# A top-32 mask made by a GpSimd compare in the first 48 slots instead of by ScalarE's bound and Relu

## The chip, the cores and the metric

The kernel runs on one core of a Trainium2 chip. Five engines work side by side: TensorE (PE in the profile; PEld is its weight load), VectorE (DVE), ScalarE (ACT), GpSimd (POOL) and SyncE (SP, which only issues transfers here). The metric is the device time of one execution in microseconds (us). The kernel before took 1338.02 us in the median of three runs (1337.96 to 1338.56).

## The reference

Two blocks follow each other. The first is attention over 8 batches, 8 heads, 576 positions and 64 columns per head, in which each row keeps only its 32 largest scores:

```
scores = scale * q @ k.T                        # 576 x 576 per head
kth    = the 32nd largest score of each row
scores = where(scores >= kth, scores, -1e9)
attn   = exp(scores - max(scores));  attn /= sum(attn) + 1e-9
out    = attn @ v
```

The outputs of all heads are laid side by side (4608 rows of 512). The second block is a mixture of 8 experts: each row goes to the one expert with the largest gate logit, `relu(x @ w1[e]) @ w2[e]`, and the result is multiplied by the gate's probability.

## The kernel before, in words

**Slots.** The attention is cut into 144 slots, 18 per batch. A slot holds two tiles (m = 0 and 1) of 128 query rows by 576 keys. The loop `loop()` goes through the slots; in each of them every engine gets its instructions in the order in which the loop writes them (TensorE, ScalarE and VectorE by a manual schedule, GpSimd by `in_turn`). Four units of two heads make a batch.

**The work of one slot**, with the lines of the kernel before:

- TensorE multiplies q and k (L292) and ScalarE copies the scores out into the tile `s`, 128x2x576 (L299). This is done three slots ahead (`AHEAD = 3`); `s` has four buffers.
- VectorE finds the 32 largest of each row. For the *next* slot it folds the 576 scores into halves by a pairwise maximum and minimum, `h` (L306) and `l` (L308), and later once more, `few` (L314) and `hl` (L316). These four are TENSOR_TENSOR operations with two inputs. `search()` then takes the eight largest of the set-aside parts (L345), and four rounds of MAX8 and MATCH_REPLACE8 (L354, L362) on the folded row give the 32 largest, `tops`. In the instruction order of VectorE, one slot goes: h, l, six MAX8 of L345, three rounds, few, hl, the last MAX8 of each of the two tiles, and then h of the next slot. The 32nd value, `thr = tops[:, :, 31]`, is the row's threshold.
- ScalarE turns the threshold into a bound, `low = thr * 2^120` (L371), and `depths()` makes `w = relu(low - s * 2^120)` for each of the two tiles (L387): 0 for a score that is kept, a huge number for one that isn't.
- GpSimd subtracts: `w = s - w` (`less()`, L396, two per slot). It also makes `nbias`, minus the row's maximum times the scale, behind the first round of MAX8 (L358), and `doubt` (L377), by which the fold is verified at the end.
- ScalarE takes the exponential of `w` with `nbias` as bias and adds up the row (L404). TensorE transposes it a slot later (L415), ScalarE copies that out (L422), and the product with v follows when a head pair is complete.
- When a unit is complete, GpSimd scales its rows and gate logits: xl (L487), lg (L489, L490 or L492) and x (L500). This falls into ten of the first 48 slots. At the end of a batch it scatters the rows to memory by expert (L567).

`w` has three buffers, `few` three.

**The experts.** The blocks of the second part (L893, L910) are strewn between the slots as rows arrive; the first can only start when two batches are through, after about slot 48. What is left of them runs on TensorE behind the last slot.

Of the kernel before, what the change touches and what calls it, by code (L numbers as in the profile page):

```python
# [9 lines left out]
F32 = mybir.dt.float32  # L10
I32 = mybir.dt.int32
AF = mybir.ActivationFunctionType
ALU = mybir.AluOpType
# [5 lines left out]
TOP_K = 32  # L19
NEG = -3.0e38  # L20
STEEP = 2.0 ** 120
EPS = 1e-9


# [18 lines left out]
def kernel(  # L43
# [47 lines left out]
    nc = tc.nc  # L91
    B, U, P, _ = qk.shape
# [23 lines left out]
    scale = float(D) ** -0.5  # L116
# [13 lines left out]
    k = SimpleNamespace()  # L130
# [116 lines left out]
    def in_turn(put):  # L247

        if not k.exact:
            tc.keep_in_program_order(put)  # L250
        return put
# [68 lines left out]
    def tick():  # L320

        while aside:
            if next(aside[0], "end") != "end":
                return
            aside.pop(0)
# [4 lines left out]
        if steps in aside:  # L330
            aside.remove(steps)

    def search(tiles, s, f, then=lambda: None):

        m_all = range(2)
        tops = k.small.tile([P, 2, TOP_K], F32, name="tops", bufs=4)
        if k.exact:
            src = [s[:, m, :, :].rearrange("p j k -> p (j k)") for m in m_all]
            width = S
        else:  # L340
            src = [f.few[:, m, 0:QF] for m in m_all]
            width = LW
            for m in m_all:
                for j, away in enumerate((f.l[:, m, :], f.hl[:, m, 0:QF // 2], f.hl[:, m, QF // 2:QF])):
                    nc.vector.max(out=f.few[:, m, QF + 8 * j:QF + 8 * j + 8], in_=away)  # L345
        scr = k.att.tile([P, 2, width], F32, name="scr", bufs=1)
        nbias = k.small.tile([P, 2], F32, name="nbias", bufs=3)
        R = TOP_K // 8

        for r in range(R):  # L350
            if r == R - 1:
                then()
            for m in m_all:
                nc.vector.max(out=tops[:, m, r * 8:(r + 1) * 8], in_=src[m])  # L354
                if r:
                    tick()
            if r == 0:
                in_turn(nc.gpsimd.tensor_scalar_mul(nbias, tops[:, :, 0], -scale))  # L358
            if r < R - 1:
                for m in m_all:  # L360
                    first = r == 0 and not k.exact
                    nc.vector.match_replace(  # L362
                        out=src[m] if first else scr[:, m, :], in_to_replace=tops[:, m, r * 8:(r + 1) * 8],
                        in_values=src[m], imm_value=NEG,
                    )
                    if r:
                        tick()
                    src[m] = f.few[:, m, :] if first else scr[:, m, :]
        thr = tops[:, :, TOP_K - 1]
        low = k.small.tile([P, 2], F32, name="low", bufs=3)  # L370
        nc.scalar.activation(low, thr, AF.Copy, scale=STEEP)  # L371

        def doubts():
            n, i = tiles[0]
            at = n.b * U + n.u
            over = doubt[:, at:at + 2, 2 * NC, :] if tails(tiles) else doubt[:, at, 2 * i:2 * i + 2, :]
            k.last_pool = in_turn(nc.gpsimd.tensor_tensor(  # L377
                over, f.few[:, :, QF + 7:LW:8], _inner(thr, NL), op=ALU.subtract
            )).ins

        return low, nbias, doubts

    def depths(s, low):

        w = k.att.tile([P, 2, S], F32, name="w", bufs=1 if k.exact else 3)
        for m in range(2):
            nc.scalar.activation(  # L387
                w[:, m, :], s[:, m, :, :].rearrange("p j k -> p (j k)"), AF.Relu,
                scale=-STEEP, bias=low[:, m:m + 1],
            )  # L390
        return w
# [78 lines left out]
    def divisors(n):  # L470
        rz = rz_of[n.u % 2]
        nc.scalar.activation(rz[:, 0:NT], n.z, AF.Copy, bias=EPS)
        if n.u % 2:
            nc.scalar.activation(rz[0:ST, NT:NT + 1], n.z[0:ST, NT - 1:NT], AF.Copy, bias=EPS)
            nc.scalar.activation(rz[0:ST, NT - 1:NT], n.z[ST:P, NT - 1:NT], AF.Copy, bias=EPS)
        else:
            nc.scalar.activation(rz[0:ST, NT:NT + 1], n.z[ST:P, NT - 1:NT], AF.Copy, bias=EPS)
        yield
# [59 lines left out]
    def places(r, x):  # L538
# [6 lines left out]
        def steps():  # L545
# [5 lines left out]
            yield  # L551
            nc.vector.tensor_scalar_add(den, den, EPS)
            yield
# [376 lines left out]
    FIRST = 13  # L930
    ARRIVED = 13
    AHEAD = 3
    ON_CHIP = 3
    KEEP = 3 * PIECES
    BETWEEN = 2

    with fast:
# [7 lines left out]
        per_batch = len(work) // B  # L945
# [5 lines left out]
        def landed(n):  # L951
            return clock is None or clock - n.at >= ON_CHIP

# [152 lines left out]
        got_of, s_of, f_of, w_of = {}, {}, {}, {}  # L1106
# [16 lines left out]
        def loop():  # L1123
            nonlocal credit, rate, clock
            for i in range(min(AHEAD, len(work))):
                multiply(i)
                s_of[i], steps = scores(got_of.pop(i))
                for step in steps:
                    step()
            multiply(AHEAD)  # L1130
            f_of[0] = fold(s_of[0])
            fold_on(f_of[0])
            for i, (b, g) in enumerate(work):
                tiles = tiles_of(i)
                u, tile = g[0]
                if tile == 0 and u % 2 == 0:
                    open_unit(tiles[0][0])
                if tails(tiles):
                    open_unit(tiles[1][0])

                then = lambda: None
                if i + 1 < len(work):
                    f_of[i + 1] = fold(s_of[i + 1])
                    then = lambda: fold_on(f_of[i + 1])
                low, nbias, doubts = search(tiles, s_of[i], f_of.pop(i), then)
                at_place("small")
                w_of[i] = depths(s_of[i], low)
                less(s_of.pop(i), w_of[i])
                doubts()
                put_stores()  # L1150
                scatter(1)
                at_place("pool")
                at_place("relu")
                at_place("rows")
                at = i % per_batch
                if at == FIRST and b:
                    rate = new_of[b - 1] * PIECES / (U * NT)
                credit += rate * len(g)
                room = left
                if b == B - 1 and at >= ARRIVED:  # L1160
                    room -= KEEP
                    credit = room / (len(work) - i)
                share = {0: 0.5, 1: 1.2, 2: 1.6, 3: 0.5, 2 * NC: 1.4}[tile]
                now = max(0, min(int(credit * share + 0.5), room))
                credit -= now
                clock = i
                if i + AHEAD < len(work):
                    s_of[i + AHEAD], steps = scores(got_of.pop(i + AHEAD))
                    for step in steps:
                        step()  # L1170
                evacuate()
                at_place("turn")
                turns = turning(i - 1) if i else iter(())
                next(turns, None)
                part = min(BETWEEN, now - now // 2)
                rest = pieces(part)
                next(turns, None)
                rest = pieces(now - now // 2 - part + rest)
                weights(tiles, w_of[i], nbias)
                next(turns, None)  # L1180
                evacuate()
                if i + AHEAD + 1 < len(work):
                    multiply(i + AHEAD + 1)
                if tile == NC - 1:
                    end = ending(b, u)
                    late.append([end, next(end)])
                at_place("products")
                at_place("weights")
                credit = min(credit + pieces(now // 2 + rest), 6 * rate)

            for _ in turning(len(work) - 1):
                pass
            assert len(late) == 1
            clock = None
            for place in late[0][0]:
                if place == "rows":
                    pieces(4)
            kept = left - (SURE + HALVES + PLAIN) * PIECES
            assert kept >= 0, kept
            k.apart = True  # L1200
            pieces(kept)
# [20 lines left out]
    with ExitStack() as outer:  # L1222
# [10 lines left out]
        with ExitStack() as st:  # L1233
# [7 lines left out]
            with tc.For_i(0, B, 1) as b:  # L1241
# [3 lines left out]
                for u in range(0, U, 2):  # L1245
# [4 lines left out]
                    for g in groups(u):  # L1250
                        tiles = [(two[a - u], tile) for a, tile in g]
                        s, steps = scores(products(tiles))
                        for step in steps:
                            step()
                        low, nbias, _ = search(tiles, s, None)
                        w = depths(s, low)
# [81 lines left out]
```

## Time and profile before

| | |
|---|---|
| median of three runs | 1338.02 us |
| the profiled execution | 1339.03 us, of it the span 1337.4 us |
| TensorE busy | 1189.3 us (89%) |
| VectorE busy | 1076.6 us (81%) |
| ScalarE busy | 930.8 us (70%) |
| GpSimd busy | 661.9 us (49%) |
| bound `low` (L371), 144 in the run | 216 ns mean |
| Relu `w<-s,low` (L387), 288 | 768 ns mean |
| GpSimd subtraction (L396), 288 | 1444 ns mean |

A row of a group names the line, the engine, the operation, what is written and read, the shape and the count; then the busy time in us and the mean in ns of one; then the idle time of the engine just before them and what ended it. In a timeline each row has its start and its duration in us, and x2 means two of them merged. In the table by stretches each engine has its busy time and, in brackets, its instructions; PEclk is the granted TensorE clock as a share of full speed.

### The profile page before, as it was taken

The page shows a single profiled execution, that of the slowest core. Times are in us where ns is not written, and L with a number is a line of the kernel's source. Part 1 is how long each engine was busy: PE and PEld are TensorE (multiplying, and loading weights), DVE is VectorE, ACT ScalarE, POOL GpSimd, SP SyncE. Part 2 cuts the span into 40 slices and gives each one's busy share as a digit, 9 for nine tenths or more (in the row PEclk, how much of TensorE's full clock was granted, in tenths as well). Part 3 has the DMA queues.
Part 4 walks back from the last instruction along what each step waited for, and adds up shares of the span by engine and source line. Part 5 has one row for each costly group of instructions (what it writes and reads, how often), then busy time and mean ns, then how long its engine had stood idle before and what let it go on. Part 6 is the DMA issues. An engine that isn't in the chain of part 4 may idle for free. (4 is left out here: it accounts for less than half of the span.)

```text
span 1337.4 us, 24295 instructions
## 1 busy us (share of the span) xinstructions
PE 1189.3 (89%) x7570; PEld 831.4 (62%) x7570; DVE 1076.6 (81%) x4629; ACT 930.8 (70%) x2125; POOL 661.9 (49%) x805
## 2 busy tenths in 40 slices
PE   5667766766799999999999999999999999999995
PEld 3344443444466766676677666666677667699973
DVE  7999999999999999999999999999999932000000
ACT  4788788887888888888787888887778851111110
POOL 3454547555755665567555756475547642000000
PEclk9788788888899999999999999999999999999998
DMA  2000001001384348435855294329452739946790
GB/s 84 30 29 30 30 29 65 29 29 38 122 305 168 108 164 288 160 110 175 297 208 179 74 350 170 118 76 372 171 204 87 283 116 332 369 146 219 290 342 18
DMA packets 95563, 214.36 MB, mean 160 GB/s; under 512 B 4926, under 2 KB 25662, under 8 KB 95424
## 3 DMA queue, kind: packets, MB, share of 16 engines
q1 hardware_dynamic: 88800, 192.45, 40.8%
q0 software_dynamic: 6336, 19.97, 4.2%
q8 instruction: 61, 1.00, 0.3%
q14 instruction: 78, 0.64, 0.2%
q10 hardware_dynamic: 288, 0.30, 0.1%
HBM read 191.42 MB, written 21.80 MB: 159 GB/s over the span
## 5 line engine op out<-in xcount | busy, mean ns | idle before, releaser
L396 POOL TENSOR_TENSOR w<-s,w 128x576 f32<-128x576 f32 x288 | 410.2, 1444 | 418.4 <-ACT w L387 418.4
L893 PE MATMUL ph<-xTs,w 128*128 128x128 f32 x2048 | 250.2, 276 | 5.9 <-ACT xTs L790 5.9
L893 PEld LDWEIGHTS ph<-xTs,w 128*128 128x128 f32 x2048 | 239.1, 192 | 21.9 <-issue 14.6
L910 PE MATMUL py<-w,hT 128*128 128x512 f32 x512 | 236.2, 597 | 0.0
L404 ACT ACTIVATE w<-w,nbias 128x576 f32<-128x576 f32 x288 | 224.1, 792 | 3.0 <-POOL w L396 2.0
L292 PE MATMUL sc<-qkb 64*128 64x288 f32 (+1 forms) x1280 | 206.0, 473 | 9.5 <-ACT s L299 5.1
L387 ACT ACTIVATE w<-s,low 128x576 f32<-128x576 f32 x288 | 207.6, 768 | 4.7
L415 PE MATMUL wTm<-turn,w 128*128 128x128 f32 x1152 | 170.1, 287 | 32.0 <-ACT xl L468 21.4
L415 PEld LDWEIGHTS wTm<-turn,w 128*128 128x128 f32 x1152 | 132.0, 145 | 92.5 <-issue 34.4
L299 ACT COPY s<-sc 128x576 f32<-128x576 f32 x288 | 168.9, 640 | 10.4 <-PE sc L292 10.4
L1217 DVE CAST any_i<-pd 1x1 int32<-1x1 f32 x1 | 0.1, 145 | 207.9 <-PE pd L1215 207.9
L422 ACT COPY wT<-wTm 128x512 f32<-128x512 f32 x256 | 139.2, 604 | 39.3 <-PE wTm L415 39.2
L354 DVE MAX8 tops<-scr 128x8 f32<-128x168 f32 x576 | 162.8, 317 | 0.0
L450 PE MATMUL po<-wT,vb 128*64 128x288 f32 x1024 | 154.9, 450 | 0.4 <-ACT wTt L437 0.4
L354 DVE MAX8 tops<-few 128x8 f32<-128x144 f32 (+1 forms) x576 | 154.4, 300 | 0.0
L292 PEld LDWEIGHTS sc<-qkb 64*128 64x128 f32 (+1 forms) x1280 | 110.1, 195 | 65.4 <-issue 25.6
L910 PEld LDWEIGHTS py<-w,hT 128*128 128x128 f32 x512 | 90.7, 190 | 90.4 <-issue 89.2
L808 POOL DMA_INDIRECT out_dram<-y,xg x40 | 42.6, 1066 | 189.8 <-ACT y L869 82.5
L345 DVE MAX8 few<-l 128x8 f32<-128x288 f32 x288 | 127.3, 442 | 0.0
L450 PEld LDWEIGHTS po<-wT,vb 128*64 128x64 f32 x1024 | 74.2, 150 | 77.3 <-issue 26.0
L306 DVE TENSOR_TENSOR h<-s 128x576 f32<-128x576 f32 x144 | 114.8, 797 | 3.9 <-ACT s L299 3.7
L308 DVE TENSOR_TENSOR l<-s 128x576 f32<-128x576 f32 x144 | 108.0, 750 | 0.0
(175 smaller groups left out, 1649.8 us busy)
## 6 DMA issues: line engine op xcount, KB each, us to landing
w<-in_moe_w_dram SPq DMA_DIRECT2D x72, 2048.0 KB, 8.6
qkb<-in_qk_dram SPq DMA_DIRECT2D x31, 608.0 KB, 5.8
vb<-in_v_dram SPq DMA_DIRECT2D x32, 320.0 KB, 3.1
xg<-x_rows SPq DMA_DIRECT2D x36, 257.0 KB, 10.6
x_rows<-blank SPq DMA_DIRECT2D x5, 257.0 KB
x_rows<-blank POOLq DMA_DIRECT2D x4, 257.0 KB, 8.2
x_rows<-x,posi POOLq DMA_INDIRECT x40, 3.1
out_dram<-y,xg POOLq DMA_INDIRECT x40, 4.5
```

Source lines behind the costliest of these rows:

```text
L292: nc.tensor.matmul(ps[rows, j, 0:HF], n.q[d, cols], n.k[d, keys], start=True, stop=True)
L299: lambda m=m, ps=ps: nc.scalar.copy(s[:, m, :, :], ps[:, :, 0:HF]) for m, ps in enumerate(got)
L345: nc.vector.max(out=f.few[:, m, QF + 8 * j:QF + 8 * j + 8], in_=away)
L354: nc.vector.max(out=tops[:, m, r * 8:(r + 1) * 8], in_=src[m])
L387: nc.scalar.activation(w[:, m, :], s[:, m, :, :].rearrange("p j k -> p (j k)"), AF.Relu, scale=-STEEP, bias=low[:, m:m + 1],)
L396: k.last_pool = in_turn(nc.gpsimd.tensor_tensor(w[:, m, :], s[:, m, :, :].rearrange("p j k -> p (j k)"), w[:, m, :], op=ALU.subtract)).ins
L404: nc.scalar.activation(w[:, m, :], w[:, m, :], AF.Exp, scale=scale, bias=nbias[:, m:m + 1], accum_out=n.z[:, c:c + 1])
L415: nc.tensor.transpose(pm[:, c * P:(c + 1) * P], w[:, m, first:first + P], ident)
L422: nc.scalar.copy(wT[:, :, m, q], pm4)
L450: nc.tensor.matmul(po[r, 0:HF], n.v[:, c, r], rhs, start=(c == 0), stop=(c == KC - 1))
L893: nc.tensor.matmul(ph[:, f, :], n.w1[:, 0, dt, fc * P:(fc + 1) * P], n.xT[:, dt, :], start=(dt == 0), stop=(dt == DT - 1),)
L910: nc.tensor.matmul(py, hT[:, f, :], n.w2[:, 0, f, :], start=(f == 0), stop=(f == FT - 1))
```

## The change

In slots 0 to 47 (`i < 2 * per_batch + FIRST - 1`, with 18 slots to a batch and FIRST = 13) both tiles are masked by GpSimd: one TENSOR_SCALAR per tile writes `w = (s < thr) * 2^100`, with the threshold read per row from `tops`. The bound and the two Relus on ScalarE are left out in these slots. The subtraction, the exponential and all else stay; from slot 48 on everything is as before.

```
+DEEP = 2.0 ** 100
...
-    def search(tiles, s, f, then=lambda: None):
+    def search(tiles, s, f, then=lambda: None, early=()):
...
         thr = tops[:, :, TOP_K - 1]
-        low = k.small.tile([P, 2], F32, name="low", bufs=3)
-        nc.scalar.activation(low, thr, AF.Copy, scale=STEEP)
+        low = None
+        if len(early) < 2:
+            low = k.small.tile([P, 2], F32, name="low", bufs=3)
+            nc.scalar.activation(low, thr, AF.Copy, scale=STEEP)
...
-        return low, nbias, doubts
+        return (low, thr), nbias, doubts
-    def depths(s, low):
+    def depths(s, bounds, early=()):
+        low, thr = bounds
         w = k.att.tile([P, 2, S], F32, name="w", bufs=1 if k.exact else 3)
         for m in range(2):
+            if m in early:
+                in_turn(nc.gpsimd.tensor_scalar(
+                    w[:, m, :], s[:, m, :, :].rearrange("p j k -> p (j k)"), thr[:, m:m + 1], DEEP,
+                    ALU.is_lt, ALU.mult,
+                ))
+                continue
             nc.scalar.activation(
                 w[:, m, :], s[:, m, :, :].rearrange("p j k -> p (j k)"), AF.Relu,
                 scale=-STEEP, bias=low[:, m:m + 1],
             )
...
+    EARLY = (0, 1)
...
-                low, nbias, doubts = search(tiles, s_of[i], f_of.pop(i), then)
+                early = EARLY if i < 2 * per_batch + FIRST - 1 else ()
+                low, nbias, doubts = search(tiles, s_of[i], f_of.pop(i), then, early)
                 at_place("small")
-                w_of[i] = depths(s_of[i], low)
+                w_of[i] = depths(s_of[i], low, early)
```

## The prediction

> **What bounds the kernel now.** I read the busy time by stretches first, since the change touches only slots 0 to 47.
>
> ```profile
> core 0: us, PE busy (x) PEld busy (x) DVE busy (x) ACT busy (x) POOL busy (x), PEclk, DMA share, GB/s
> 20.00:100.00 80.00, 54.84 (x307) 32.39 (x309) 79.99 (x348) 63.80 (x148) 39.36 (x53) 0.85 0.10 32
> 180.00:260.00 80.00, 57.02 (x345) 34.09 (x341) 80.00 (x348) 66.10 (x157) 47.88 (x56) 0.87 0.16 52
> 390.00:420.00 30.00, 29.59 (x204) 20.16 (x203) 30.00 (x132) 26.10 (x62) 19.06 (x23) 1.00 0.54 186
> ```
>
> The first two rows lie in the changed slots: VectorE (DVE) has no idle time, ScalarE (ACT) a fifth, GpSimd (POOL) half. The third row lies behind them: VectorE and TensorE are both full there, and after 1110 us TensorE alone is. So ScalarE's time is worth nothing in the first 360 us, and each microsecond by which VectorE gets longer there moves all that follows, in an order fixed by the program, by a microsecond.
>
> Next the groups of instructions by shape in 20 to 360 us, to see whether VectorE's durations are all its own.
>
> ```profile
> L306 DVE TENSOR_TENSOR h<-s 128x576 f32<-128x576 f32 x47 | 35.7, 760 | 0.0
> L314 DVE TENSOR_TENSOR few<-h 128x288 f32<-128x288 f32 x48 | 25.2, 525 | 0.0
> L371 ACT ACTIVATE low<-tops 128x2 f32<-128x2 f32 x47 | 9.7, 207 | 46.1 <-DVE tops L354 46.0
> ```
>
> The median of h is 735 ns, so its mean of 760 hides a few long ones (maximum 1329); few is about 444 in a plain slot and 525 in the mean. ScalarE waits for the row's threshold (tops) 46 us in all: it is the early one.
>
> Then the timeline of one plain slot (start, duration), from the end of one search to the start of the next but one.
>
> ```profile
> 188.50 0.56 DVE L354 MAX8 tops<-scr 128x8 f32<-128x168 f32 x2
> 188.98 0.74 DVE L306 TENSOR_TENSOR h<-s 128x576 f32<-128x576 f32 x1
> 189.10 0.20 ACT L371 ACTIVATE low<-tops 128x2 f32<-128x2 f32 x1
> 189.33 1.44 ACT L387 ACTIVATE w<-s,low 128x576 f32<-128x576 f32 x2
> 189.64 0.75 DVE L308 TENSOR_TENSOR l<-s 128x576 f32<-128x576 f32 x1
> 190.19 2.84 POOL L396 TENSOR_TENSOR w<-s,w 128x576 f32<-128x576 f32 x2 [4.34 <-ACT w L387]
> 193.00 0.19 POOL L377 TENSOR_TENSOR doubt<-few,tops 128x6 f32<-128x6 f32 x1
> 193.16 0.21 POOL L358 TENSOR_SCALAR nbias<-tops 128x2 f32<-128x2 f32 x1
> 194.69 0.45 DVE L314 TENSOR_TENSOR few<-h 128x288 f32<-128x288 f32 x1
> 195.05 0.45 DVE L316 TENSOR_TENSOR hl<-h 128x288 f32<-128x288 f32 x1
> 195.42 0.56 DVE L354 MAX8 tops<-scr 128x8 f32<-128x168 f32 x2
> 195.90 0.74 DVE L306 TENSOR_TENSOR h<-s 128x576 f32<-128x576 f32 x1
> ```
>
> A slot is 6.92 us. Counted from the start of h at 188.98: h and l run to 1.41, the two subtractions on POOL go from 1.21 to 4.05, few starts at 5.71, hl ends at 6.52. POOL's reads lie between VectorE's two pairs of TENSOR_TENSOR; the bound and the two Relus on ScalarE are what put them there.
>
> Last the places where a POOL operation and one of those four meet.
>
> ```profile
> 71.99 1.26 POOL L500 TENSOR_TENSOR x<-xl,rz 128x640 f32<-128x640 f32 x1
> 72.10 1.46 DVE L314 TENSOR_TENSOR few<-h 128x288 f32<-128x288 f32 x1
> ...
> 231.40 0.73 DVE L306 TENSOR_TENSOR h<-s 128x576 f32<-128x576 f32 x1
> 231.43 2.49 POOL L500 TENSOR_TENSOR x<-xl,rz 128x640 f32<-128x640 f32 x1
> 232.06 0.74 DVE L308 TENSOR_TENSOR l<-s 128x576 f32<-128x576 f32 x1
> ```
>
> They exclude each other. At 72.10 POOL had begun to read: few took 1.46 instead of 0.44, until 0.31 after POOL's end at 73.25, so VectorE loses POOL's end minus its own start minus about 0.12. At 231.43 h was first by 0.03: POOL's 1.26 became 2.49, ending 1.12 behind l. VectorE lost nothing, and POOL got in only behind both h and l. At 330.88 POOL's x began 0.14 ahead of few at 331.02 and still lost to few and hl, so the side that wins is settled near the start of the VectorE operation, within about a tenth.
>
> **The change part by part.** Removed in each of 48 slots: the bound (0.20) and two Relus (0.77 each), 1.75 us of ScalarE. VectorE does not wait for ScalarE in 20 to 360 us (0.6 us in all), so this is worth 0; it covers itself, as the scores that VectorE reads are copied three slots ahead.
>
> Added in each slot: two compares (128x576, one tile in, a scalar per row) on POOL, ahead of the two subtractions, 96 in all. The order of VectorE's instructions stays as it is. The first compare waits for the first tile's last MAX8 alone, the second for the second's.
>
> Their duration T has no row. Below: a memset goes from 522 ns at 513 columns to 817 at 864, 0.84 ns per element, and a COPY of 128x128 takes 289, so one stream over 576 is at least 0.18 + 576 x 0.83 ns = 0.66. Above: the subtraction of the same shape, two tiles in, 1.42. One tile is read here as in the COPY, so I stay near the lower end and add some for two operations: T = 0.80. By the Trainium skill, GPSIMD Engine Reference, section Elementwise, a body of at most two operations costs 1.03 cycles per element and a tight loop about 1.8, from which I estimate 0.5 or 0.9 us without the start; no row here shows it.
>
> Where they fall: the first MAX8 of the pair at 195.42 ends at 195.74, 0.16 ahead of h. POOL started 0.10 behind its release when idle (nbias at 14.15 in the first slot, its MAX8 pair ended at 14.05), and an extra wait instruction stands before the compare. So the compare starts 0.06 ahead of h to level with it. Rows on either side: x at 0.14 ahead of few lost, x at 0.11 ahead of few won, x at 0.03 behind h lost to h and l. I take it that h wins, being nearest to the last row. Then the first compare ends at 1.41 - 0.14 + 0.80 = 2.07 (0.14 of start-up is hidden while it waits: 1.26 against 1.12), the second at 2.84, the subtractions at 5.66. The cover ends at few: 5.71 plus 0.12. **Plain slots: 0.** The cover is gone from T = 0.89 on (4.06 + 2T > 5.83): each 0.1 more costs 0.2 a slot, or nearly 10 us over 48. T = 1.42 would cost 48 x 1.07 = 51.
>
> Queued behind the compares on POOL are the subtractions, for which the exponential waits, then doubt, nbias and, in ten slots, the row products (xl 0.33, lg 0.27 or 0.54, x 1.26) and the scatters. The exponential started 4.85 into the slot above; the first subtraction is then done at 4.24, the second at 5.66 against a need at 5.62: 0. The scatters of rows come up to 3 us later; the first block that reads them lands slots later: 0. The buffers of s, w and few are three or four deep, against a delay of 1.6 us: 0. No DMA of SP is moved.
>
> **The ten slots with row products:** today POOL's x ends up on few in most of them; few and h lose 48 x (525 - 444) + 47 x (760 - 735) ns = 5.1 us in 20 to 360, about 0.5 each. With POOL clear at 5.66 instead of 4.05 these products start at 5.85, wait behind few and hl (6.52) and run into the next h or l, where x costs up to 1.26 - 0.12 = 1.1. Difference 10 x 0.6 = 6 us, and 1 us for doubt touching few in the plain slots.
>
> Sum: 0 + 0 + 6 + 1 = +7 us. The profiled execution took 1339.03 (span 1337.4 and 1.6 around it), 1 above the median of 1338.02, from which I count: 1345.
>
> At this point a rule is weighed against the rows. The Trainium skill, SBUF — State Buffer, section Who interferes with whom, says that a VectorE instruction with two SBUF inputs contends with a GpSimd instruction that reads SBUF, and that whoever comes first has the shared port for the whole instruction while the other blocks. The trace agrees (1.46 and 2.49 above), but by the rule alone POOL would come in between h and l, and l would wait T - 0.18 in every slot, +30 us; the row at 231.43 shows h and l passing together, +0. Perfetto Trace Analysis, section Optimizing Scalar/DVE Operations, speaks against the change too: moving work between the two may not help as they share a read port.
>
> **The rivals.** (a) The compare wins against h. Then h waits 0.80 - 0.06 - 0.12 = 0.62, the second compare follows directly, comes in behind h and holds up l by 0.8 - 0.18 = 0.62: 48 x 1.24 = +60, 1398 (T = 0.66 gives +46, T = 1.42 +119). For it: x at 0.11 ahead won. Against: every POOL operation that I found starting less than 0.04 ahead of one of the four, or behind it, left it untouched. (b) h wins but l does not: 48 x 0.62 = +30, 1368. For it: small products that began 0.07 or more into an h that had itself waited came in ahead of l. (c) h wins, but T is above 0.89: +10 at T = 0.92, +28 at 1.1, up to +58 (51 and 7). For it: two operations and a compare, for which no row speaks. (d) The other side: the row products slide so far that x starts level with the next h, as at 231.43, and waits behind both; then the 5.1 us that VectorE loses today are gone: 1333. It decides if T lies between 0.75 and 0.85 and doubt, xl and lg fit in ahead of h; but nbias and the next two compares queue behind x and are then late themselves. (e) The row products cost as much as today, so the change isn't seen: 1338 to 1340.
>
> **How the numbers follow.** Forecast (h and l pass, T under 0.89) 0.36: +3 to +12. (c) 0.22, (a) 0.20, (b) 0.08, (e) 0.10, (d) 0.04. The range starts at 1338, which leaves (d) out, and ends at 1398, (a) with T = 0.8, which leaves out the slower half of (a): 0.14 in all. The likeliest case has 1341 to 1350. A measurement of this kernel tells about 0.2% (2.7 us) from no change: faster 0.04 (d), same 0.12 ((e) and the lowest edge of the forecast), slower 0.84.
>
> **What would show it.** In 20 to 360 us: compares of about 0.80 on POOL, the first recorded longer (about 2.1, as it waits through h and l); h and l unchanged at 735 and 746; few's mean within 30 ns of 525; slots of 6.92. Case (a) shows h and l both near 1.35, (b) l alone, (c) few above 0.6 in plain slots. ScalarE's busy time falls by 84 us, and no VectorE wait for it appears. From slot 48 on the two traces run alike, shifted by one constant. I am wrong if that shift is under 3 or over 12 us, and most likely by who wins at h, or by T.

## The result and the profile after

The changed kernel takes 1436.59 us against 1337.99 us for the kernel before in the same runs, a ratio of 1.073 (95% interval 1.072 to 1.075): 98.6 us slower. The forecast was 1345 with a range of 1338 to 1398. The profiled execution has a span of 1435.2 us, 97.8 more than before.

Where the time came in is read from the start of VectorE's h in both traces, slot by slot:

| h of slot | 8 | 16 | 24 | 32 | 40 | 48 | 60 | 100 | 143 |
|---|---|---|---|---|---|---|---|---|---|
| before, us | 59.5 | 116.6 | 174.6 | 231.4 | 287.5 | 346.7 | 431.9 | 735.6 | 1065.8 |
| changed, us | 69.7 | 139.9 | 209.4 | 283.8 | 357.7 | 432.6 | 531.0 | 834.7 | 1165.0 |
| later by, us | 10.2 | 23.3 | 34.9 | 52.4 | 70.3 | 85.9 | 99.2 | 99.2 | 99.2 |

Most of it arises in the 48 changed slots and 13 us in the next twelve, while GpSimd works off what they left; from slot 60 the shift is constant to the end.

Three groups of instructions of GpSimd and ScalarE in 20 to 455 us of the changed kernel:

```profile
L392 POOL TENSOR_SCALAR w<-s,tops 128x576 f32<-128x576 f32 x96 | 221.6, 2308 | 12.3 <-DVE tops L355 3.5 <-DVE past L643 0.3
L406 POOL TENSOR_TENSOR w<-s,w 128x576 f32<-128x576 f32 x95 | 143.9, 1535 | 3.8
L414 ACT ACTIVATE w<-w,nbias 128x576 f32<-128x576 f32 x94 | 72.9, 776 | 197.1 <-POOL w L406 197.1
```

The compare costs 2.31 us in the mean (2.21 the shortest and 2.22 the median), where the forecast had 0.80 and an upper end of 1.42. ScalarE, freed of its Relus, waits 197 us for GpSimd's subtractions.

The changed kernel's busy time by stretches:

```profile
core 0: us, PE busy (x) PEld busy (x) DVE busy (x) ACT busy (x) POOL busy (x), PEclk, DMA share, GB/s
20.00:100.00 80.00, 49.20 (x207) 27.69 (x207) 80.00 (x284) 34.06 (x79) 77.67 (x56) 0.83 0.06 20
300.00:420.00 120.00, 81.95 (x394) 47.81 (x396) 100.47 (x410) 61.69 (x149) 115.71 (x96) 0.73 0.08 27
```

GpSimd, half idle before, is full in both. VectorE is full in the first row, too, yet it does 284 instructions in 80 us where it did 348 before; in the second row it is idle for 19.5 us of 120. So the loss has two forms. In the first, a GpSimd operation and one of VectorE's two-input operations h, l, few and hl want to read at the same time and one waits for the other (a meeting, below); it is alone in the first 100 us. In the second, VectorE stands idle as GpSimd has more work in a slot than VectorE (a floor, below). The first is seen in a timeline of the changed kernel at slot 8:

```profile
64.45 4.52 POOL L392 TENSOR_SCALAR w<-s,tops 128x576 f32<-128x576 f32 x2
68.46 0.44 DVE L315 TENSOR_TENSOR few<-h 128x288 f32<-128x288 f32 x1
68.82 0.45 DVE L317 TENSOR_TENSOR hl<-h 128x288 f32<-128x288 f32 x1
69.05 3.36 POOL L406 TENSOR_TENSOR w<-s,w 128x576 f32<-128x576 f32 x2
69.67 1.47 DVE L307 TENSOR_TENSOR h<-s 128x576 f32<-128x576 f32 x1
71.07 1.96 DVE L309 TENSOR_TENSOR l<-s 128x576 f32<-128x576 f32 x1
72.37 0.72 POOL L380 TENSOR_TENSOR doubt<-few,tops 128x6 f32<-128x6 f32 x1
73.06 0.23 POOL L359 TENSOR_SCALAR nbias<-tops 128x2 f32<-128x2 f32 x1
73.39 2.22 POOL L392 TENSOR_SCALAR w<-s,tops 128x576 f32<-128x576 f32 x1
```

GpSimd goes from one slot's compares (64.45) to the next's (73.39) without a gap, 8.94 us against a slot of 6.92 before. Its subtractions, released by its own compares now, land on h and l, which take 1.47 and 1.96 instead of 0.74 and 0.75. The compare itself does not hold VectorE up: few and hl run inside it at 0.44 and 0.45. Later on GpSimd is the last of all, and h and l are nearly undisturbed while VectorE waits. What ended VectorE's waits in 20 to 455 us of the changed kernel (us, times, longest; in 20 to 360 us before it waited 0.6 us):

```profile
DVE h L307 <- ACT s L300: 25.4, 20, 4.1
DVE rz L489 <- ACT rz L485: 18.2, 5, 4.7
DVE few L315 <- POOL doubt L380: 7.9, 5, 4.6
```

The scores and the sums come late as ScalarE stands waiting for the subtractions in front of them. Added up over the rows of both traces up to slot 48, h, l, few and hl take 22 us more than before, VectorE stands idle 58 us more, and some 6 us fall on its small operations: the waiting is two thirds of the 86. Over the whole run VectorE is busy 30.7 us longer (1107.3 against 1076.6), and the span grew by 97.8, so its idle time grew by 67.1.

### The profile page after: what moved, and what is told of

The parts are those of the page before. It is cut to its first block, busy times and chain, and to the rows that moved or that the text cites. A ratio compares the mean times of both kernels' runs of the same rounds, so it can differ in the third digit from the quotient of the medians.

```text
span 1435.2 us, 24299 instructions
## 1 busy us (share of the span) xinstructions
PE 1239.1 (86%) x7570; PEld 853.2 (59%) x7570; DVE 1107.3 (77%) x4629; ACT 862.6 (60%) x1981; POOL 902.3 (63%) x901
## 5 line engine op out<-in xcount | busy, mean ns | idle before, releaser
L406 POOL TENSOR_TENSOR w<-s,w 128x576 f32<-128x576 f32 x288 | 419.5, 1477 | 264.7 <-ACT w L397 260.7
L425 PE MATMUL wTm<-turn,w 128*128 128x128 f32 x1152 | 187.0, 305 | 71.4 <-ACT w L414 36.4
L392 POOL TENSOR_SCALAR w<-s,tops 128x576 f32<-128x576 f32 x96 | 221.6, 2308 | 12.3 <-DVE tops L355 3.5
L425 PEld LDWEIGHTS wTm<-turn,w 128*128 128x128 f32 x1152 | 142.9, 154 | 138.0 <-ACT w L414 47.9
L293 PE MATMUL sc<-qkb 64*128 64x288 f32 (+1 forms) x1280 | 216.0, 497 | 6.5 <-DMA qkb<-in_qk_dram 5.5
L460 PE MATMUL po<-wT,vb 128*64 128x288 f32 x1024 | 162.9, 468 | 3.6 <-ACT wTt L445 3.2
L293 PEld LDWEIGHTS sc<-qkb 64*128 64x128 f32 (+1 forms) x1280 | 114.3, 205 | 66.4 <-issue 30.6
L307 DVE TENSOR_TENSOR h<-s 128x576 f32<-128x576 f32 x144 | 122.5, 851 | 33.8 <-ACT s L300 33.7
L397 ACT ACTIVATE w<-s,low 128x576 f32<-128x576 f32 x192 | 138.4, 768 | 3.1
L460 PEld LDWEIGHTS po<-wT,vb 128*64 128x64 f32 x1024 | 77.8, 158 | 87.6 <-issue 44.9
```

The source lines that it names most:

```text
L293: nc.tensor.matmul(ps[rows, j, 0:HF], n.q[d, cols], n.k[d, keys], start=True, stop=True)
L392: in_turn(nc.gpsimd.tensor_scalar(w[:, m, :], s[:, m, :, :].rearrange("p j k -> p (j k)"), thr[:, m:m + 1], DEEP, ALU.is_lt, ALU.mult,))
L397: nc.scalar.activation(w[:, m, :], s[:, m, :, :].rearrange("p j k -> p (j k)"), AF.Relu, scale=-STEEP, bias=low[:, m:m + 1],)
L406: k.last_pool = in_turn(nc.gpsimd.tensor_tensor(w[:, m, :], s[:, m, :, :].rearrange("p j k -> p (j k)"), w[:, m, :], op=ALU.subtract)).ins
L425: nc.tensor.transpose(pm[:, c * P:(c + 1) * P], w[:, m, first:first + P], ident)
L460: nc.tensor.matmul(po[r, 0:HF], n.v[:, c, r], rhs, start=(c == 0), stop=(c == KC - 1))
```

## The experiments

The kernels that leave work out send rows to other experts; of them, only what lies up to slot 48 is compared unless the text says more. A run given without a ratio is a single execution. Sums of what h, l, few and hl take more than before are added up over the rows of the traces, up to slot 48.

### One tile instead of two

```
-    EARLY = (0, 1)
+    EARLY = (0,)
```

> Only tile 0 of each of the first 48 slots is masked by GpSimd; tile 1 keeps the bound and the Relu on ScalarE. Theory A (GpSimd is the longest engine with two compares of 2.21 us): its own work falls from 8.3 to 2.21 + 2.82 + 0.4 + 0.7 = 6.1 us a slot, below VectorE's 6.9, so nearly all of the loss is gone: 1338 to 1350 us, what is left being meetings in the slots with row products. Theory B (VectorE is held up at the shared port by each compare and subtraction): half of the compares leave half of the loss, about 1387 us.

Measured: 1374.15 us, ratio 1.027 (1.025 to 1.029), about 36 us lost; between the two expectations, and neither is right. VectorE is never idle (80.0 of 80 us in 20 to 100, 100.0 of 100 in 260 to 360), so GpSimd's work is no floor here. The timeline of this kernel shows the cause:

```profile
186.25 0.74 DVE L307 TENSOR_TENSOR h<-s 128x576 f32<-128x576 f32 x1
186.26 3.40 POOL L392 TENSOR_SCALAR w<-s,tops 128x576 f32<-128x576 f32 x1 [0.32 <-DVE tops L355]
186.91 0.75 DVE L309 TENSOR_TENSOR l<-s 128x576 f32<-128x576 f32 x1
189.75 2.77 POOL L406 TENSOR_TENSOR w<-s,w 128x576 f32<-128x576 f32 x2
191.96 0.88 DVE L315 TENSOR_TENSOR few<-h 128x288 f32<-128x288 f32 x1
```

The compare begins 0.01 behind h and waits through h and l, as the forecast had it; it ends 3.41 into the slot, the subtractions at 6.27, and few, which starts at 5.71, has to wait for them. The mean of few in 20 to 360 us is 882 ns, against 525 before. Up to slot 48, which starts 33.5 us later, few takes 16 us more and h, l and hl 10 together; most of the rest falls on VectorE's small operations for the gates and the rows' places. The forecast's own chain with one compare (1.41 - 0.14 + T, then two subtractions) gives 6.3 for T = 2.21.

### Compares without subtractions

```
-                less(s_of.pop(i), w_of[i])
+                s = s_of.pop(i)
+                if not early:
+                    less(s, w_of[i])
```

The compare writes 1 instead of 2^100 here, so that the exponential stays finite.

> Both compares stay, the two subtractions are left out in the first 48 slots (the exponential then takes the mask itself, so the attention of these slots is not computed). Theory A: GpSimd has 4.42 + 0.4 + 0.7 = 5.5 us a slot, VectorE is the longest again and h of slot 48 starts at 347 to 352 us (before 346.7, changed 432.5). Theory B with the compares as what holds VectorE up: h or l stay above 0.9 us in the mean and slot 48 starts beyond 380 us.

Measured: h of slot 48 starts at 343.4 us, 3.3 us *earlier* than in the kernel before and 3.6 below the expected 347 to 352. h, l, few and hl have means of 736, 780, 448 and 446 ns in slots 1 to 47. Ninety-six compares of 2.21 us beside VectorE cost nothing; as the subtractions are gone, the slots with row products meet few no longer (448 against 528). A stretch of this kernel:

```profile
179.28 0.73 DVE L307 TENSOR_TENSOR h<-s 128x576 f32<-128x576 f32 x1
179.29 5.58 POOL L392 TENSOR_SCALAR w<-s,tops 128x576 f32<-128x576 f32 x2 [0.69 <-PE rank L544]
179.94 0.74 DVE L309 TENSOR_TENSOR l<-s 128x576 f32<-128x576 f32 x1
```

The first compare waits for h and l, then both run to 5.59 into the slot and leave VectorE's next operations as they were.

### The subtraction straight behind the threshold

```
-                in_turn(nc.gpsimd.tensor_scalar(
-                    w[:, m, :], s[:, m, :, :].rearrange("p j k -> p (j k)"), thr[:, m:m + 1], DEEP,
-                    ALU.is_lt, ALU.mult,
-                ))
+                k.last_pool = in_turn(nc.gpsimd.tensor_tensor(
+                    w[:, m, :], s[:, m, :, :].rearrange("p j k -> p (j k)"), _inner(thr[:, m], S), op=ALU.subtract,
+                )).ins
```

with `less()` left out as in the run above.

> No compare and no Relu in the first 48 slots: GpSimd subtracts the row's threshold (broadcast, so two inputs) straight from the scores, one operation per tile; the mask is left out. It tests who wins at h when a reading GpSimd operation is released by the last MAX8 of tile 0. As forecast (h and l pass together): h at 735 and l at 746 ns in the median, slot 48 starts at 345 to 352 us. Rival (a) (GpSimd wins): h and l both about 1.0 us longer, slot 48 near 440 us. Rival (b): l alone longer, near 395 us. It also shows that ScalarE's 1.75 us a slot are worth nothing, if slot 48 does not start before 345 us.

Measured: slot 48 starts at 350.4 us, 3.7 later than before; the medians of h and l are 735 and 748 ns. A plain slot:

```profile
188.32 2.42 POOL L392 TENSOR_TENSOR w<-s,tops 128x576 f32<-128x576 f32 x1 [3.64 <-DVE tops L355]
188.33 0.74 DVE L307 TENSOR_TENSOR h<-s 128x576 f32<-128x576 f32 x1
188.99 0.75 DVE L309 TENSOR_TENSOR l<-s 128x576 f32<-128x576 f32 x1
```

GpSimd's start is recorded 0.01 ahead of h, and h and l still pass together. In eight of 47 slots, with the same recorded start, GpSimd came in between h and l and l lost 0.95 each, 7.6 us in all; what sets these eight apart is open. The forecast's step on who wins at h is confirmed for an operation with two inputs as well, and its step on l in 39 of 47 slots. ScalarE lost 1.75 us of work in each slot and nothing came earlier, so that work was worth nothing.

### The cost of the operation by itself

Slots 0 to 47 take eight forms in turn; the new ones in the place of the compare:

```
+                if form == 0:
+                    in_turn(g.tensor_scalar(wm, sm, t, DEEP, ALU.is_lt, ALU.mult))
+                elif form == 1:
+                    in_turn(g.tensor_scalar(wm, sm, t, None, ALU.is_lt))
+                elif form == 2:
+                    in_turn(g.tensor_scalar(wm, sm, t, 1.0, ALU.mult, ALU.mult))
+                elif form == 3:
+                    in_turn(g.tensor_scalar(wm, sm, 0.0, 1.0, ALU.is_lt, ALU.mult))
+                elif form == 4:
+                    in_turn(g.tensor_scalar(wm[:, 0:HF], sm[:, 0:HF], t, DEEP, ALU.is_lt, ALU.mult))
+                    in_turn(g.tensor_scalar(wm[:, HF:S], sm[:, HF:S], t, DEEP, ALU.is_lt, ALU.mult))
+                elif form == 5:
+                    in_turn(g.tensor_scalar(wm, sm, t, 0.0, ALU.subtract, ALU.max))
+                elif form == 6:
+                    in_turn(g.tensor_copy(wm, sm))
+                else:
+                    in_turn(g.tensor_scalar(wm, sm, t, None, ALU.mult))
```

> Measures the compare by itself: slots 0 to 47 take eight forms in turn on GpSimd, both tiles alike: compare and multiply with the row's threshold as now; compare alone; multiply and multiply; compare and multiply with constants; two halves of 288 columns; subtract and maximum; a copy; one multiply. Most of them leave the mask out. If the cost goes by the number of operations, one operation takes about 1.2 us and two take 2.2; if the compare is the dear part, multiply and multiply takes 0.7 to 1.1; if the scalar per row is, the form with constants does. The halves tell the fixed part: 2 x (0.2 + 1.0) if 0.2 is fixed. The copy is expected at 0.66 to 0.70.

Measured: the lines of this kernel's trace by source line, in the order of the forms (count; shortest, median and longest in ns; first and last start). The longest ones had to wait for h and l.

```profile
L395 POOL TENSOR_SCALAR w<-s,tops x12: 2207/2225/3483, 17.8 to 364.3; 128x576 f32<-128x576 f32 x12
L397 POOL TENSOR_SCALAR w<-s,tops x12: 1712/1719/1726, 28.4 to 372.9; 128x576 f32<-128x576 f32 x12
L399 POOL TENSOR_SCALAR w<-s,tops x12: 734/744/1927, 35.4 to 380.3; 128x576 f32<-128x576 f32 x12
L401 POOL TENSOR_SCALAR w<-s x12: 2128/2142/2808, 41.2 to 386.3; 128x576 f32<-128x576 f32 x12
L404 POOL TENSOR_SCALAR w<-s,tops x12: 1247/1248/1251, 52.4 to 401.2; 128x288 f32<-128x288 f32 x12
L406 POOL TENSOR_SCALAR w<-s,tops x12: 2195/2210/2237, 60.6 to 410.1; 128x576 f32<-128x576 f32 x12
L408 POOL COPY w<-s x12: 652/662/667, 69.5 to 418.1; 128x576 f32<-128x576 f32 x12
L410 POOL TENSOR_SCALAR w<-s,tops x12: 1715/1730/2907, 74.8 to 425.6; 128x576 f32<-128x576 f32 x12
```

None of the three expectations holds by itself. The compare is not the dear part: one multiply alone costs 1.73 us, as much as one compare (1.72), and subtract with maximum costs 2.21, as much as compare with multiply. A second operation adds 0.49. The scalar per row is not it either (constants: 2.14). Multiply with multiply takes a fast way, 0.74, near the copy's 0.66; it is the one form of these that does. From the halves, the slow way has a fixed part of 2 x 1.248 - 2.21 = 0.29 us and 3.3 ns for each column.

### The change with an operation of 0.74 us

```
-                    w[:, m, :], s[:, m, :, :].rearrange("p j k -> p (j k)"), thr[:, m:m + 1], DEEP,
-                    ALU.is_lt, ALU.mult,
+                    w[:, m, :], s[:, m, :, :].rearrange("p j k -> p (j k)"), thr[:, m:m + 1], 1.0,
+                    ALU.mult, ALU.mult,
```

> The changed kernel with multiply and multiply in place of compare and multiply in the first 48 slots (the same shape and the same scalar per row; the mask is left out), which took 0.74 us by itself against 2.21. If only the compare's duration was wrong in the forecast, all else of it holds here: h and l at 735 and 746 ns in the median, few at 446, and h of slot 48 starts at 348 to 357 us (346.7 before, 3 to 10 us from meetings in the slots with row products). If moving the mask to GpSimd costs by itself, through the port or the later release, slot 48 starts beyond 375 us.

Measured: slot 48 starts at 355.9 us, 9.1 later than before, within the expected 348 to 357; the medians of h, l and few are 734, 745 and 443 ns. The whole execution takes 1347.83 us and has as many instructions as the changed kernel. This is the forecast's case, with its duration:

```profile
182.97 0.73 DVE L307 TENSOR_TENSOR h<-s 128x576 f32<-128x576 f32 x1
182.97 2.72 POOL L392 TENSOR_SCALAR w<-s,tops 128x576 f32<-128x576 f32 x2 [1.11 <-DVE tops L355]
183.62 0.74 DVE L309 TENSOR_TENSOR l<-s 128x576 f32<-128x576 f32 x1
185.67 2.76 POOL L406 TENSOR_TENSOR w<-s,w 128x576 f32<-128x576 f32 x2
188.39 0.20 POOL L380 TENSOR_TENSOR doubt<-few,tops 128x6 f32<-128x6 f32 x1
188.57 0.24 POOL L359 TENSOR_SCALAR nbias<-tops 128x2 f32<-128x2 f32 x1
189.66 0.44 DVE L315 TENSOR_TENSOR few<-h 128x288 f32<-128x288 f32 x1
```

The two operations wait through h and l and end at 2.72, the subtractions at 5.46 into the slot, before few starts.

### VectorE's order swapped, one tile and both

For the changed slots, few and hl go between the last two MAX8:

```
-            if r == R - 1:
+            if r == R - 1 and not early:
                 then()
             for m in m_all:
                 nc.vector.max(out=tops[:, m, r * 8:(r + 1) * 8], in_=src[m])
+                if r == R - 1 and early and m == 0:
+                    then()
```

> One tile on GpSimd as in the run with one tile, and in the first 48 slots VectorE's few and hl are put between the last MAX8 of tile 0 and that of tile 1, not ahead of both. The compare is then released ahead of hl's end and should begin to read before h asks for the port. Theory C (one tile lost 36 us since the compare lost to h and l, ended 1.41 us late and pushed the subtractions onto few): the compare ends near 1.9 us into the slot, few is back at 0.45 us, 1338 to 1350 us. If the loss comes from GpSimd's load or from ScalarE, it stays near 1374 us.

Measured: 1360.12 us, ratio 1.017 (1.015 to 1.018): 14 of the 36 us are gone, not all of them. The compare ends 1.9 us into the slot as expected, but h is now held up in most slots (its median is 1046 ns; in 26 of 47 it takes over 1 us):

```profile
187.49 2.65 POOL L394 TENSOR_SCALAR w<-s,tops 128x576 f32<-128x576 f32 x1 [1.37 <-DVE tops L355]
187.61 0.44 DVE L317 TENSOR_TENSOR hl<-h 128x288 f32<-128x288 f32 x1
188.22 1.05 DVE L307 TENSOR_TENSOR h<-s 128x576 f32<-128x576 f32 x1
189.19 0.74 DVE L309 TENSOR_TENSOR l<-s 128x576 f32<-128x576 f32 x1
190.23 2.78 POOL L408 TENSOR_TENSOR w<-s,w 128x576 f32<-128x576 f32 x2
```

The compare gets in when hl ends at 188.05, and h, from 188.22, loses 0.31. By the forecast's rule (loss = end of the exclusion - start - 0.12) GpSimd let go at about 188.65, 0.6 after it got in, while it worked on to 190.14. The traces of seven kernels with the compare, taken together, show the same. Where it had not been held up itself and no other kind of GpSimd operation began, h or few starting less than 0.6 behind its start took up to 0.46 us longer (28 cases), and of the 272 h, l, few and hl that started later inside it none took over 0.03 longer. Up to slot 48, which still starts 20 us later than in the kernel before, h takes 7.5 us more, few 6 and hl 3.5; few is still long in 21 of 47 slots.

> The same swap of VectorE's order in the changed kernel, both tiles on GpSimd. Theory A (GpSimd's own work, 4.42 + 2.82 + 0.4 + 0.7 = 8.3 us a slot, is the floor): h of slot 48 starts at 405 to 425 us (432.5 as changed), still at least 58 us behind the kernel before. If the meetings at h and l are the cause, it starts near 350 us.

Measured: h of slot 48 starts at 435.4 us, no better than the changed kernel's 432.6, and 10 beyond the upper end of theory A; the whole is 1439.91 us. What h and l take more than before falls from 19 us to 8, and what few and hl take more rises from 3 to 19. So the swap moves the meetings, and that those at h and l alone are the cause is out. VectorE's idle time stays: 98.1 us busy of 120 in 300 to 420 us.

### Every second slot

```
-                early = EARLY if i < 2 * per_batch + FIRST - 1 else ()
+                early = EARLY if i < 2 * per_batch + FIRST - 1 and i % 2 else ()
```

> Both tiles are masked by GpSimd in every second of the first 48 slots only (24 slots, 48 compares, as many as with one tile in each). Theory A (GpSimd's work is the floor, and the buffers carry a long slot into a short one): a pair of slots holds 8.4 + 4.0 = 12.4 us of GpSimd's work against 13.8 of VectorE's, so most of the loss is gone: 1345 to 1375 us, what is left being subtractions that meet h, l, few or hl. If the loss were paid per compare, half of it stays, 1387 us.

Measured: 1393.28 us, ratio 1.041 (1.039 to 1.043), 54 us lost. Theory A misses it; half the slots with two compares cost more than all slots with one. VectorE is nearly never idle (79.3 of 80 us in 180 to 260), and GpSimd has time left (71.1). Two compares push the subtractions across hl and onto the next h and l:

```profile
189.49 4.54 POOL L392 TENSOR_SCALAR w<-s,tops 128x576 f32<-128x576 f32 x2
193.13 0.44 DVE L315 TENSOR_TENSOR few<-h 128x288 f32<-128x288 f32 x1
193.50 0.44 DVE L317 TENSOR_TENSOR hl<-h 128x288 f32<-128x288 f32 x1
194.11 3.27 POOL L406 TENSOR_TENSOR w<-s,w 128x576 f32<-128x576 f32 x2
194.35 1.77 DVE L307 TENSOR_TENSOR h<-s 128x576 f32<-128x576 f32 x1
196.04 1.95 DVE L309 TENSOR_TENSOR l<-s 128x576 f32<-128x576 f32 x1
```

In this slot h loses 1.03 and l 1.20; in most of the 24 it is 0.74 and 1.20. Up to slot 48, which starts 48 us later, h, l, few and hl take 40 us more than before and VectorE stands idle for 6. Here the meetings are most of the loss, nearly without a floor.

### Four compares, no subtraction

```
+                for _ in range(2):
                     in_turn(nc.gpsimd.tensor_scalar(
```

added to the run without subtractions, so each compare is made twice.

> The run without subtractions, with each compare made twice (four of 2.21 us a slot in the first 48 slots, no subtraction; the attention of these slots is not computed). No two-input GpSimd operation of that size is left to meet h, l, few and hl. Theory A (GpSimd's own work is a floor of its own, beside the meetings): 8.84 + 0.4 + 0.7 = 9.9 us a slot, h of slot 48 starts at 460 to 490 us with h and l near 740 ns and VectorE idle for the difference. If only meetings at the port cost time, it starts near 343 us, as with two compares.

Measured: slot 48 starts at 502.6 us, 156 later than before and somewhat beyond the expected 460 to 490. In this kernel's busy time by stretches VectorE stands idle beside a full GpSimd:

```profile
300.00:400.00 100.00, 60.96 (x262) 35.76 (x262) 64.59 (x272) 39.61 (x95) 97.31 (x66) 0.63 0.09 29
```

Of the 156 us VectorE stands idle for 146; h, l, few and hl take 2 us more than before. So GpSimd's work is a floor of its own, once it is longer than VectorE's slot. Both forms of the loss exist nearly apart: meetings with little of a floor (every second slot), a floor with hardly a meeting (four compares).

### The row products one slot later

An edit of the kernel before, to see what a meeting in the slots with row products is worth:

```
             logits(n, lg)
+            if u < U - 1 and b < 2:
+                yield "rows"
             rows(n, x)
```

> The kernel before with one move: in the first two batches, for three of four units, the scaling of the rows (x) is put one slot behind that of the logits in GpSimd's order, so that it runs between doubt and few instead of on few. If the meetings in the slots with row products cost VectorE what the forecast counted (5.1 us in ten slots), some 4 us go: 1333 to 1335 us; if they cost nothing, 1338 us. The result is that of the kernel before.

Measured: 1335.77 us against 1337.89, ratio 0.9983 (0.9974 to 0.9992), 2.1 us faster, half of the 4 us expected and 0.8 above the expected stretch; slot 48 starts 3.1 us earlier. In this kernel's 20 to 360 us few takes 486 ns in the mean instead of 525:

```profile
L314 DVE TENSOR_TENSOR few<-h 128x288 f32<-128x288 f32 x48 | 23.3, 486 | 0.0
```

It is a little faster than both kernels of this case, and it keeps the mask on ScalarE.

> The kernel before with the scaling of the rows one slot later in all eight batches, not the first two alone. Behind slot 48 TensorE is full as well as VectorE, so VectorE's gain there should not add up: 1334 to 1336 us as with two batches. If VectorE alone decides there too, another 6 us or more go: below 1330 us.

Here the same is done without `and b < 2`. Measured: 1336.85 against 1338.87 us, ratio 0.9989 (0.9980 to 0.9998). Behind slot 48 the gain does not add up, as expected of a stretch in which TensorE is full as well; 1336.85 lies 0.85 above the expected stretch, with a kernel before that is 1 us above its usual median in the same runs.

## Why the prediction was wrong

**What failed: T, and its upper bound.** The forecast put the compare at 0.80 us between 0.66 (a stream of one input) and 1.42 (the subtraction with two inputs). It takes 2.21. The upper end was taken from an operation of another kind on the ground that it reads more; but reading is not what costs here. Reading and writing 576 columns takes 0.66 us in the copy, and the scalar operations other than multiply with multiply spend 1.7 to 2.2 us whatever they compute. Two rows of a different operation do not bound a third, and the trace had no GpSimd TENSOR_SCALAR wider than two columns. The estimates from the Trainium skill (GPSIMD Engine Reference, section Elementwise), 0.5 or 0.9 us without the start, miss the compare as well: the runs show 3.3 ns per column for it, 1.9 us without the start. The lower one is near the copy and multiply with multiply (0.66 and 0.74 with the start).

**What held.** With an operation of nearly the forecast's duration (multiply and multiply, 0.74 us), the same change ends at 1347.83 us and slot 48 comes 9.1 us later, where the forecast said +7 and 1345. Most of its steps hold one by one: h wins against the compare released by tile 0's MAX8, and l passes with it (the run with one tile; the direct subtraction in 39 of 47 slots); the removed 1.75 us of ScalarE are worth 0; the operations end where the chain 4.06 + 2T puts them (5.46 seen, 5.54 for 0.74); the slots with row products cost a few us. That 9.1 is so near to 7 is in part luck: h, l, few and hl took 4.2 us more than before, and some 5 us fell on VectorE's small operations for the gates and the rows' places (oh 2.4, slot_i and ci 1.0 each), which the forecast didn't count. The sign was right, and T was one of the two likeliest failures that it named, but the range was closed with the false upper bound: rival (c) ended at +58, its largest T being 1.42.

**What the forecast could not have got right with T alone.** Its price beyond T = 0.89, 0.2 us a slot for each 0.1, would make 48 x 2.65 = 127 us at 2.21, and 98.6 were measured. The formula let a GpSimd operation exclude VectorE from its start to its end. For the subtraction and x that is so; the compare lets go after about 0.6 us, and few and hl run inside it undisturbed. And it had no floor: 4.42 for the compares, 2.82 for the subtractions, 0.4 for doubt and nbias and 0.7 for row products and scatters are 8.3 us a slot, more than VectorE's 6.92, so after some ten slots of meetings at h and l (means of 1.41 and 1.82 us in 20 to 100 us) VectorE waits on GpSimd instead (h 0.82 and l 0.76 in 300 to 420). With it failed the 0 for the buffers, reckoned against a delay of 1.6 us, as GpSimd's slot of 8.94 adds 2 us to the delay each time, and the sign that no VectorE wait for ScalarE appears: h waited 25.4 us for scores that ScalarE copies.

**What stays open.** GpSimd's cycle is 8.9 us or more (9.1 in the mean of slots 8 to 48), not 8.3, and 10.7 with four compares, not 9.9; its own waits for h and l (a doubt of 0.72, a pair of subtractions of 3.36) make up some of it, and how much of the rest is due to the port wasn't separated. Why multiply with multiply is fast and a single multiply isn't, no run here tells.

The rule of the Trainium skill in SBUF — State Buffer, section Who interferes with whom, that the one that comes first has the port for its whole instruction, is only half confirmed: the two-input subtraction does so (l 1.95 beside it), the compare with one input does not, beyond its first 0.6 us.

## What to carry to other kernels

Before work is moved to an idle engine, measure the very form of instruction there; neither a neighbour with more inputs nor a simpler one bounds it. Then add up the engine's whole work in a slot, and look where its other instructions are pushed: here the compares cost nothing without the subtractions, and the subtractions hardly met anything in the kernel before; both in one slot cost 86 us up to slot 48. Relieving an engine for which the fullest one does not wait (VectorE waited 0.6 us for ScalarE in 20 to 360) gains nothing.

## What the runs showed of the hardware that was not expected

- GpSimd's TENSOR_SCALAR over 128x576 takes 1.72 to 1.73 us with one operation and 2.14 to 2.22 with two, but 0.74 with multiply and multiply; a copy takes 0.66.
- A running GpSimd compare leaves VectorE's two-input operations alone after its first 0.6 us or so (few 0.44 and hl 0.45 inside it; 272 of 272 cases), while a subtraction holds them until it ends (l 1.95 instead of 0.75).
- VectorE's h and l, back to back, mostly keep a GpSimd operation out for both if its recorded start is level with that of h, be it 0.01 ahead: the compares of the run with one tile that began 0.01 behind h took 3.40 instead of 2.21, h and l 0.74 and 0.75. In eight of 47 slots of the direct subtraction it came in between them.
